# The last block's second layer as two column halves, each with its own finish and store

## The chip, the cores and the metric

The kernel runs on one core of a Trainium2 chip. The metric is the device time of one execution in microseconds (us), smaller is better. The core has a matrix engine (PE in the profile, with its weight loads listed apart as PEld), a vector engine (DVE), a scalar engine (ACT), a third elementwise engine that also issues loads (POOL), and a sync engine (SP) that here only issues DMA transfers. Each engine works through its own list of instructions in order; the lists meet at semaphores.

## The reference

Inputs are q, k and v of shape 4 x 8 x 768 x 64 (batch, heads, positions, head width) and the weights of one feed-forward layer. What is computed, cut to its core:

```python
scores = q @ k.T / sqrt(64)                       # per batch and head
keep   = (key < 4) | (0 <= query - key < 128)     # 4 sink keys, and a window of 128
a      = softmax(where(keep, scores, -1e9))
x      = (a @ v), heads side by side              # [4, 768, 512]
xn     = (x - mean(x)) / sqrt(var(x) + 1e-6) * g_ln
out    = x + relu(xn @ w_ch1) @ w_ch2             # 512 -> 2048 -> 512, float32
```

## The kernel before

The 4 x 768 positions are cut into 24 blocks of 128 rows, numbered t = 0 to 23. Each block goes through attention, and its normalized rows are laid out transposed in `xnt`. Four blocks make a group, so there are six groups, g = 0 to 5. For a group the feed-forward part has two layers:

- `m1` (the first layer): 16 tiles of 128 hidden units. Each takes four matmuls of 512 columns (the 512 rows of the group; group 0 does it in two parts of 256) into a PSUM bank `ph`, and one relu by ACT or DVE into a bf16 tile `h`.
- `m2` (the second layer): for each of the four blocks of the group, 16 matmuls that add up in one PSUM bank `pc` of 128 x 512 float32. A matmul takes a 128 x 128 piece of `h` as its weights and streams 512 columns of `w2s`. The 16 are added to the plan in four quanta of four. After them comes `fin`, one DVE instruction (scalar_tensor_tensor: `pc` times the row's factor `rsg`, plus the attention output `xt`) into the float32 tile `ot`, and `store`, one DMA of 256 KB that SP issues to the output.

The order of work is not written by hand. Every step is added to a `Planner` with a cost for each engine that could take it, its dependences, the buffers it takes and drops, and a priority; `plan.run` simulates this and picks the engine, the order on it and the buffer slots. Only the resulting order is issued; the costs are not times of the chip. PSUM banks come from a ring `pa` of four, output tiles from a ring `ot` of four.

At the end of the program nothing but group 5's second layer is left: blocks 20, 21, 22 and 23, one after the other on PE. After the last store SP waits, one instruction after the other, for each semaphore that its DMAs and the other engines have used; then the engines meet at a barrier and the program ends. Stores take eight DMA semaphores in rotation, and block 23's store is on the one that SP waits for second.

Lines of the profile that the text below uses: L603 the first layer's matmuls, L617 and L619 its relu on DVE and ACT, L634 the second layer's matmuls, L646 `fin`, L653 `store`, L517 the attention output's scaling (another scalar_tensor_tensor from PSUM, of 256 columns), L729 the program's end.

Of the kernel before, what the change touches and what calls it, by code (L numbers as in the profile page):

```python
# [7 lines left out]
FP32 = mybir.dt.float32  # L8
# [3 lines left out]
ALU = mybir.AluOpType  # L12
# [117 lines left out]
def kernel(  # L130
# [12 lines left out]
    nc = tc.nc  # L143
# [5 lines left out]
    DM = moe_w_ch1.shape[0]  # L149
    DH = moe_w_ch1.shape[1]  # L150
    NH1 = DH // 128
    NDM = DM // 128
    NT = B * RB
# [13 lines left out]
    plan = Planner(RINGS)  # L167
# [7 lines left out]
    def buf(ring, slot, shape, dtype, name):  # L175
        return pools[ring].tile(shape, dtype, name=name, tag=f"{ring}{slot}")

    def bank(slot, name):
        return buf("pa", slot, [128, 512], FP32, name)
# [14 lines left out]
    w2s = consts.tile([128, NH1, DM], BF16, name="w2s")  # L194
# [12 lines left out]
    xt = [consts.tile([128, DM], BF16, name=f"xt_{t}") for t in range(NT)]  # L207
# [50 lines left out]
    def rows_of(t):  # L258
        b, r = divmod(t, RB)
        return b, slice(128 * r, 128 * (r + 1))  # L260
# [23 lines left out]
    d_w1, d_w2 = {}, {}  # L284
# [28 lines left out]
    P = {}  # L313
# [13 lines left out]
    qkT, vs_t, E, ES, xc, xnt, mvg, rsg = {}, {}, {}, {}, {}, {}, {}, {}  # L327
    d_c, d_xn, d_rs, d_ks, d_vs = {}, {}, {}, {}, {}
# [253 lines left out]
    quanta = []  # L582
# [3 lines left out]
    h1 = {}  # L586
    d_h1 = {}
# [38 lines left out]
    def m2(g, base):  # L626
        m = None
        for ti, t in enumerate(GROUPS[g]):
            for qt in range(4):
                def f(e, *s, qt=qt, ti=ti, t=t):  # L630
                    if s:
                        P["pc", t] = bank(s[0], "pc")
                    for ht in range(4 * qt, 4 * qt + 4):
                        nc.tensor.matmul(P["pc", t], lhsT=h1[g, ht][:, 128 * ti:128 * (ti + 1)], rhs=w2s[:, ht, :],  # L634
                                         start=(ht == 0), stop=(ht == NH1 - 1))

                m = plan.add({"PE": .865}, [m, d_w2[qt]] + [d_h1[g, ht, t] for ht in range(4 * qt, 4 * qt + 4)], f,
                             (1, base, 4 * ti + qt), take=[("pa", ("pc", t), 1)] if qt == 0 else [],
                             drop=[("h1", g, ht) for ht in range(4 * qt, 4 * qt + 4)])

                quanta.append(m)

            def fin(e, s, ti=ti, t=t):
                ot = buf("ot", s, [128, DM], FP32, "ot")
                P["ot", t] = ot
                nc.vector.scalar_tensor_tensor(ot, in0=P["pc", t], scalar=rsg[g][:, ti:ti + 1], in1=xt[t],  # L646
                                               op0=ALU.mult, op1=ALU.add)

            o = plan.add({"DVE": .75}, [m, d_rs[g]], fin, (0, t, 9), take=[("ot", ("ot", t), 1)], drop=[("pc", t)])

            def store(e, t=t):
                bb, rows = rows_of(t)
                nc.sync.dma_start(out[bb, rows, :], P["ot", t])  # L653

            plan.add({"SP": .35}, [o], store, (0, t, 9), drop=[("ot", t)], land=.66)

    SPLIT = set(range(8))
    SPLIT_S = set(range(4))
# [26 lines left out]
    for i, (layer, g) in enumerate(SEQ):  # L685
        mark[layer, g] = len(quanta)
        (m1(g, i, SUBS.get(g)) if layer == 1 else m2(g, i))
# [46 lines left out]
```

## Time and profile before

| | us |
|---|---|
| median of 5 runs | 227.85 (227.63 to 227.87) |
| the profiled execution, its time | 227.87 |
| its span in the trace | 225.83 |
| PE busy | 219.0 (97% of the span) |
| DVE busy | 135.4 (60%) |
| ACT busy | 104.0 (46%) |
| POOL busy | 76.0 (34%) |

The profiled execution took 2.04 us more than the span that its instructions cover. The granted clock of PE is full (0.999) over the span. In the profile's views a group of instructions is shown with its count, its busy time and the mean duration of one; a matmul's duration runs from its start to the end of its result, so consecutive matmuls overlap, and the distance from start to start is the smaller number.

### The profile page before, as it was taken

How to read it: one execution, taken by the hardware profiler on the slowest of the kernel's cores; microseconds unless marked ns; L12 is line 12 of the kernel's file. 1: busy time of each engine (PE TensorE's matmuls, PEld its weight loads, DVE VectorE, ACT ScalarE, POOL GpSimd, SP SyncE). 2: the span in 40 equal slices, each digit the busy share in tenths (PEclk: the TensorE clock that was granted, in tenths of full speed). 3: DMA queues.
4: the chain of work that ended last, by engine and by line, in shares of the span. 5: the costliest groups of instructions: out<-in, count | busy, mean ns of one | idle time of the engine just before them, and what ended most of it. 6: DMA issues, size and time to landing. Idle time of an engine off the chain costs nothing.

```text
span 225.8 us, 4810 instructions
## 1 busy us (share of the span) xinstructions
PE 219.0 (97%) x1948; PEld 121.2 (54%) x1948; DVE 135.4 (60%) x398; ACT 104.0 (46%) x166; POOL 76.0 (34%) x92
## 2 busy tenths in 40 slices
PE   8999999999999999999999999999999999999992
PEld 7765887655455554454555544454554544444440
DVE  5787998789577988864756773744854712100121
ACT  2377788344368641166651247632077600376000
POOL 7994275691595241933089000100000010000000
PEclk9999999999999999999999999999999999999999
DMA  7999999999999999999979996203221021200111
GB/s 44 134 158 205 183 183 206 169 180 188 195 159 140 141 139 199 169 192 183 92 96 157 177 168 120 56 8 111 69 50 23 3 70 46 93 0 3 46 67 72
DMA packets 108709, 26.52 MB, mean 117 GB/s; under 512 B 101520, under 2 KB 105616, under 8 KB 108688
## 3 DMA queue, kind: packets, MB, share of 16 engines
q0 software_dynamic: 79104, 13.64, 81.0%
q1 hardware_dynamic: 29584, 12.59, 30.0%
q8 instruction: 15, 0.25, 0.4%
q14 instruction: 6, 0.05, 0.1%
HBM read 27.27 MB, written 6.29 MB: 149 GB/s over the span
## 4 chain that ended last, share of the span: by engine, by line
PE 82%; DMA 7%; POOL 5%; DVE 4%; issue 1%; ACT 0%; POOLq 0%; ACTq 0%
PE ph L603 35%; PE pc L634 34%; PE ps L406 5%; DMA w1s<-in_moe_w_ch_dram 4%; DMA qkT<-qkn 3%; PE po L501 2%; PE po L504 2%; POOL qkn L267 2%; PE po L496 2%; POOL qkn L272 2%; POOL vn L275 2%; PE pk L413 1%; DVE w1s L299 1%; PE pt L347 1%; DVE xt L517 1%
## 5 line engine op out<-in xcount | busy, mean ns | idle before, releaser
L603 PE MATMUL ph<-xnt,w1s 128*128 128x512 bf16 (+1 forms) x448 | 90.1, 349 | 0.4 <-DVE h L617 0.2
L634 PE MATMUL pc<-w2s,h 128*128 128x512 bf16 x384 | 88.6, 379 | 0.0
L619 ACT ACTIVATE h<-ph 128x512 bf16<-128x512 f32 (+1 forms) x84 | 45.9, 546 | 53.6 <-PE ph L603 53.2
L603 PEld LDWEIGHTS <-w1s 128*128 128x128 bf16 x448 | 41.5, 98 | 35.5 <-DVE w1s L299 0.6
L634 PEld LDWEIGHTS <-h 128*128 128x128 bf16 x384 | 35.8, 98 | 39.1
L435 ACT ACTIVATE e<-ps 128x1024 bf16<-128x1024 f32 (+1 forms) x48 | 43.7, 951 | 12.5 <-PE ps L406 12.5
L646 DVE SCALAR_TENSOR_TENSOR ot<-pc,rsg,xt 128x512 f32<-128x512 f32 x24 | 17.9, 747 | 38.9 <-PE pc L634 38.9
L548 POOL TENSOR_TENSOR rsg<-ve,eps_half 128x4 f32<-128x4 f32 x6 | 6.2, 1028 | 82.2 <-DVE ve L546 82.2
L267 POOL DMA_DIRECT2D qkn<-in_q_dram x24 | 22.1, 921 | 14.8 <-DMA qkT<-qkn 12.9
L444 DVE TENSOR_TENSOR e<-e,mask_std 128x1024 bf16<-128x1024 bf16 x28 | 18.9, 683 | 10.9 <-ACT e L435 10.9
L617 DVE TENSOR_SCALAR h<-ph 128x512 bf16<-128x512 f32 (+1 forms) x28 | 15.8, 569 | 13.7 <-PE ph L603 13.7
L272 POOL DMA_DIRECT2D qkn<-in_k_dram x24 | 21.8, 910 | 3.3 <-DMA w1s<-in_moe_w_ch_dram 1.8
L275 POOL DMA_DIRECT2D vn<-in_v_dram x24 | 22.0, 920 | 1.7 <-DMA w1s<-in_moe_w_ch_dram 1.7
L517 DVE SCALAR_TENSOR_TENSOR xt<-po,rc 128x256 bf16<-128x256 f32 x48 | 20.4, 424 | 1.7
L501 PE MATMUL po<-vn,e 128*128 128x65 bf16 x192 | 17.1, 193 | 0.0
L537 DVE BATCH_NORM_STATS2 st<-xt 128x6 f32<-128x512 bf16 x24 | 16.4, 683 | 0.0
L406 PEld LDWEIGHTS <-qkT 64*128 64x128 bf16 x352 | 9.9, 94 | 10.5 <-issue 7.8
L482 ACT ACTIVATE es<-pk 128x256 bf16<-128x256 f32 x16 | 6.1, 383 | 19.9 <-PE pk L413 19.8
L514 DVE RECIPROCAL rc<-po 128x4 f32<-128x4 f32 x48 | 8.5, 177 | 11.2 <-PE po L504 10.4
L406 PE MATMUL ps<-qkT 64*128 64x128 bf16 x352 | 14.7, 218 | 0.5 <-DMA qkT<-qkn 0.5
L501 PEld LDWEIGHTS <-e 128*128 128x128 bf16 x192 | 14.0, 97 | 2.1 <-DVE e L444 0.4
L504 PE MATMUL po<-vn,e 128*128 128x65 bf16 x160 | 14.9, 193 | 0.0
(66 smaller groups left out, 146.8 us busy)
## 6 DMA issues: line engine op xcount, KB each, us to landing
out_dram<-ot SPq DMA_DIRECT2D x24, 256.0 KB, 2.4
qkn<-in_q_dram POOLq DMA_DIRECT2D x24, 128.0 KB, 7.0
qkn<-in_k_dram POOLq DMA_DIRECT2D x24, 128.0 KB, 6.8
vn<-in_v_dram POOLq DMA_DIRECT2D x24, 128.0 KB, 7.4
w1s<-in_moe_w_ch_dram POOLq DMA_DIRECT2D x4, 512.0 KB, 10.8
w2s<-in_moe_w_ch_dram POOLq DMA_DIRECT2D x4, 512.0 KB, 10.7
qkT<-qkn SPq DMA_TRANSPOSE x16, 7.2
xnt<-xc SPq DMA_TRANSPOSE x16, 5.4
```

What stands on the lines that cost most here:

```text
L267: nc.gpsimd.dma_start(qn[t][:, 0], q[b, :, rows, :].rearrange("h p d -> p h d"))
L272: nc.gpsimd.dma_start(qn[t][:, 1], k[b, :, rows, :].rearrange("h p d -> p h d"))
L275: nc.gpsimd.dma_start(vn[:, t, :, 0:64], v[b, :, rows, :].rearrange("h p d -> p h d"))
L406: nc.tensor.matmul(ps[:, h2, hh, kb, :], lhsT=qkT[t - kb][rows, 1, hp, :], rhs=qkT[t][rows, 0, hp, :], start=(hh == 0 and kb == 0 and t no ...
L435: nc.scalar.activation(E[t, half][:, :, :, 0:nkb, :], P["ps", t, half][:, :, :, 0:nkb, :], AF.Exp, scale=scale)
L444: nc.vector.tensor_mul(ee[:, :, 0:w], ee[:, :, 0:w], m[:, 0:w].unsqueeze(1).to_broadcast([128, 4, w]))
L501: nc.tensor.matmul(po[:, hh, :], lhsT=ee[:, h % 2, hh // 2, 0, :], rhs=vn[:, t, h, :], start=(r < 2 and hh == 0), stop=(r == 0), skip_grou ...
L504: nc.tensor.matmul(po[:, hh, :], lhsT=ee[:, h % 2, hh // 2, 1, :], rhs=vn[:, t - 1, h, :], start=False, stop=True, skip_group_check=True)
L517: nc.vector.scalar_tensor_tensor(xt[t][:, 256 * half:256 * half + 256].rearrange("p (h d) -> p h d", h=4), in0=po[:, :, 0:64], scalar=1.0, ...
L603: nc.tensor.matmul(ph, lhsT=w1s[:, j, 128 * ht:128 * (ht + 1)], rhs=xnt[g][:, j, cols], start=(j == 0), stop=(j == NDM - 1))
L619: nc.scalar.activation(o, i, AF.Relu)
L634: nc.tensor.matmul(P["pc", t], lhsT=h1[g, ht][:, 128 * ti:128 * (ti + 1)], rhs=w2s[:, ht, :], start=(ht == 0), stop=(ht == NH1 - 1))
```

## The change

Only block 23, the last of all, is treated differently. Its 512 output columns are computed as columns 0 to 255 and then columns 256 to 511. Each half has its own PSUM bank, its own 16 matmuls of 256 columns (the same 16 weight tiles are loaded a second time), its own `fin` of 128 x 256 and its own store of 128 KB (128 rows of 1 KB each). Both halves write into the same `ot` tile, side by side. For all other blocks `halves` has one entry and the instructions are the same.

```diff
     def m2(g, base):
         m = None
         for ti, t in enumerate(GROUPS[g]):
-            for qt in range(4):
-                def f(e, *s, qt=qt, ti=ti, t=t):
+
+            halves = [(0, DM)] if t < NT - 1 else [(0, DM // 2), (DM // 2, DM)]
+            for c0, c1 in halves:
+                cols = slice(c0, c1)
+                for qt in range(4):
+                    def f(e, *s, qt=qt, ti=ti, t=t, cols=cols):
+                        if s:
+                            P["pc", t, cols.start] = bank(s[0], "pc")
+                        for ht in range(4 * qt, 4 * qt + 4):
+                            nc.tensor.matmul(P["pc", t, cols.start][:, cols], lhsT=h1[g, ht][:, 128 * ti:128 * (ti + 1)],
+                                             rhs=w2s[:, ht, cols], start=(ht == 0), stop=(ht == NH1 - 1))
+
+                    m = plan.add({"PE": .865 / len(halves)}, [m, d_w2[qt]] + [d_h1[g, ht, t] for ht in range(4 * qt, 4 * qt + 4)], f,
+                                 (1, base, 4 * ti + qt), take=[("pa", ("pc", t, c0), 1)] if qt == 0 else [],
+                                 drop=[("h1", g, ht) for ht in range(4 * qt, 4 * qt + 4)] if c1 == DM else [])
+
+                    quanta.append(m)
+
+                def fin(e, *s, ti=ti, t=t, cols=cols):
                     if s:
-                        P["pc", t] = bank(s[0], "pc")
...
+                        P["ot", t] = buf("ot", s[0], [128, DM], FP32, "ot")
+                    nc.vector.scalar_tensor_tensor(P["ot", t][:, cols], in0=P["pc", t, cols.start][:, cols],
+                                                   scalar=rsg[g][:, ti:ti + 1], in1=xt[t][:, cols],
+                                                   op0=ALU.mult, op1=ALU.add)
+
+                o = plan.add({"DVE": .75 / len(halves)}, [m, d_rs[g]], fin, (0, t, 9),
+                             take=[("ot", ("ot", t), len(halves))] if c0 == 0 else [], drop=[("pc", t, c0)])
+
+                def store(e, t=t, cols=cols):
+                    bb, rows = rows_of(t)
+                    nc.sync.dma_start(out[bb, rows, cols], P["ot", t][:, cols])
+
+                plan.add({"SP": .35}, [o], store, (0, t, 9), drop=[("ot", t)], land=.66 / len(halves))
```

In the instruction lists of the two kernels nothing else differs: ACT and POOL have the same instructions in the same order, PE has 16 more weight loads and matmuls at its end, DVE one more instruction, SP one more store. The first matmul of the second half carries a wait for a DVE semaphore, as its bank was block 20's `pc`. The second half's store is on the DMA semaphore that SP waits for third at the program's end, the first half's on the one that it waits for second.

More of the change, by code (lines that the diff above doesn't have):

```diff
@@ L628, in m2 @@
         for ti, t in enumerate(GROUPS[g]):
-            for qt in range(4):
-                def f(e, *s, qt=qt, ti=ti, t=t):
-                    if s:
-                        P["pc", t] = bank(s[0], "pc")
[L633 to L653, printed above, removed]
@@ L655, in m2 @@
-            plan.add({"SP": .35}, [o], store, (0, t, 9), drop=[("ot", t)], land=.66)
+            halves = [(0, DM)] if t < NT - 1 else [(0, DM // 2), (DM // 2, DM)]
[13 more added lines that the diff above has]
+                def fin(e, *s, ti=ti, t=t, cols=cols):
+                    if s:
+                        P["ot", t] = buf("ot", s[0], [128, DM], FP32, "ot")
[8 more added lines that the diff above has]
+                plan.add({"SP": .35}, [o], store, (0, t, 9), drop=[("ot", t)], land=.66 / len(halves))
```

## The prediction

> **What bounds the kernel now.** I began with the chain of waits that ended last, cut to the program's end, since the change touches nothing before block 23. Its columns are start, length and what ran (us).
>
> ```profile
> 199.86 7.99 PE ph L603 x37
> 207.85 13.83 PE pc L634 x64
> 221.67 0.02 issue
> 221.70 0.75 DVE ot L646
> ```
>
> PE is the bound up to 221.70. It streams all 64 matmuls of group 5's second layer without a gap: 13.83 us / 64 = 216 ns from start to start. After 221.70 PE has nothing left, and everything is one chain: `fin` (0.75), the store, SP's last waits, the barrier. The next view is the store's line in the last 4 us, with the time from issue to landing, and SP's instructions of the program's end right after that landing.
>
> ```profile
> L653 SPq DMA_DIRECT2D out_dram<-ot x1: 332/332/332, 222.5 to 222.5; - x1
> DMA to landing us min/median/max: 2.0/2.0/2.0
> ```
>
> ```profile
> L729 SPq EVENT_SEMAPHORE  x8: 27/28/28, 224.5 to 224.9; - x8
> L729 SPq DRAIN  x2: 7/7/7, 225.0 to 225.1; - x2
> ```
>
> So the tail is: `fin` 221.70 to 222.45, issue at 222.48, landing at 224.48, eight waits of SP from 224.50 to 224.93 (0.43 us / 7 = 61 ns apart), then the barrier until 225.83. From the last matmul's end to the program's end are 4.13 us in which PE does nothing. Inside the store's 2.0 us the DMA view of 222.4 to 226 us (40 slices of 0.09 us; busy share of the DMA engines in tenths, then GB/s) shows when data moves:
>
> ```profile
> DMA  0000000000899999951000000000000000000000
> GB/s 0 0 0 0 0 0 0 0 0 0 296 410 432 364 364 387 410 205 46 0 0 0 0 0 0 0 0 0 0 0 0 0 0 0 0 0 0 0 0 0
> DMA packets 144, 0.26 MB, mean 73 GB/s; under 512 B 16, under 2 KB 16, under 8 KB 144
> ```
>
> Data moves in slices 10 to 18, 223.30 to 224.11. Before it 0.82 us pass with nothing moving, after it 0.37 us. Only the middle part depends on the size. Last, the groups kept apart by shape, for the prices (busy us, mean ns of one):
>
> ```profile
> L634 PE MATMUL pc<-w2s,h 128*128 128x512 bf16 x384 | 88.6, 379 | 0.0
> L603 PE MATMUL ph<-xnt,w1s 128*128 128x256 bf16 x128 | 16.5, 273 | 0.4 <-DVE h L617 0.2
> L634 PEld LDWEIGHTS <-h 128*128 128x128 bf16 x384 | 35.8, 98 | 39.1
> L646 DVE SCALAR_TENSOR_TENSOR ot<-pc,rsg,xt 128x512 f32<-128x512 f32 x24 | 17.9, 747 | 38.9 <-PE pc L634 38.9
> L517 DVE SCALAR_TENSOR_TENSOR xt<-po,rc 128x256 bf16<-128x256 f32 x48 | 20.4, 424 | 1.7
> L617 DVE TENSOR_SCALAR h<-ph 128x512 bf16<-128x512 f32 x16 | 10.9, 685 | 13.5 <-PE ph L603 13.5
> L617 DVE TENSOR_SCALAR h<-ph 128x256 bf16<-128x256 f32 x12 | 5.0, 415 | 0.2 <-PE ph L603 0.2
> ```
>
> **The change, part by part.**
>
> *Matmuls (path).* 16 matmuls of 512 columns become 32 of 256. The trace has 256-column matmuls with a new weight tile each, in group 0's first layer. In the timeline (start, length):
>
> ```profile
> 26.88 2.78 PE L603 MATMUL ph<-xnt,w1s 128*128 128x256 bf16 x24 [0.20 <-DVE h L617]
> ...
> 29.49 0.39 PE L347 MATMUL pt<-ident,qkn 128*128 128x128 bf16 x4
> ```
>
> 24 of them fill 26.88 to 29.49: 109 ns from start to start, although each has its own weight load of 98 ns. The loads just fit under the streaming. So 32 x 109 = 3.49 us replace 16 x 216 = 3.46 us: +0.03. The last matmul starts later than its predecessor of before by about the 0.107 us that it is shorter in duration (379 against 273 ns), so PE's end moves only by that 0.03, to 221.73. From below I allow 0; from above see the third rival.
>
> *The first half (hidden).* Its `fin` can start 1.74 us (16 x 109) after block 22's result, at about 219.99, and takes under 0.5 us. DVE is free then: block 22's `fin` runs 218.24 to 218.99. Its store is issued at about 220.5, by an SP with nothing else to do, moves data at about 221.3 to 221.7 and lands by about 222.5 even at the full store's 2.0 us. The cover is the second half's matmuls (1.74 us) and its `fin`. The second half's store would issue at about 222.2 and move its first byte 0.82 us later, at 223.0, so the two transfers do not meet. Without this cover the halves' tails would be paid one after the other.
>
> *The wait at the second half's first matmul.* It waits for DVE to have emptied its bank. This is block 20's bank, emptied at 212.1 (its `fin` starts at 211.39), some 7.5 us earlier: 0. Queued behind it on PE are the last 15 matmuls, and for these the final `fin` and store wait, so a wait that really held would be paid in full (second rival).
>
> *The last `fin` (path).* 747 ns for 512 columns; for 256 no row has this form. The other scalar_tensor_tensor that reads PSUM, L517, takes 424 at 256 columns. L617 loses 270 ns from 512 to 256 columns; off 747 that leaves 477. I take the middle, 450: -0.30, with -0.27 and -0.33 as ends.
>
> [...] In the trace the fixed part shows, since L617 at half the columns still costs 61%. [...]
>
> *The last store (path).* 128 packets of 2 KB become 128 of 1 KB on the same 16 engines, eight each. Before, eight took about 0.70 us (the stage of 0.81 less its ragged ends), 88 ns each. If the rate of some 390 GB/s holds, 1 KB takes 44 ns and the saving is 8 x 44 = 0.35. If a packet has a fixed part it is less: the profile's queue table gives the hardware queue 29584 packets in 30.0% of 16 engines' span, 1084 us. The 24 stores' 3072 packets at 88 ns take 270 of these, so that the other 26,100, of 241 bytes on average, took 31 ns each. Between 31 ns at 241 bytes and 88 at 2048, 1 KB comes to 56 ns: a saving of 8 x 32 = 0.26. I take -0.30. As no row has 1 KB packets on this queue, the far end is 0.
>
> [...]
>
> *SP's last waits (path).* The final landing now releases the third of SP's waits instead of the second; the second, for the first half's store, is over by then. One step of 61 ns fewer stands after the landing: -0.06 (0 if the order does not matter).
>
> *The sum.* +0.03 - 0.30 - 0.30 - 0.06 = -0.63 us. Against the profiled execution's own time, 225.83 span + 2.04 around it = 227.87, this gives 227.24; that execution lay 0.02 above the median of the runs, so 227.22. The ends: 0 - 0.33 - 0.35 - 0.06 = -0.74 (227.11), and 0.03 - 0.27 - 0 - 0 = -0.24 (227.61).
>
> **The rivals.** *The store's half saves nothing*: if 1 KB packets take as long as 2 KB ones, or if landing goes from these 2.0 us to the 2.4 that is the median of all 24 stores, the tail keeps its transfer, and the sum is -0.33 to 0, 227.5 to 227.85. For it: no such packet in the trace. Against: small packets on this queue are plainly shorter, and the slower landings are in stages where loads and transposes run, while the tail has none.
>
> *The second half waits for the first's `fin`*: if the bank were not free, PE would stand for that `fin` plus the drain of the last matmul, 0.45 + (0.273 - 0.109) = 0.61, and the sum is -0.02: no change, 227.83. Against: the bank is block 20's.
>
> *Slower*: the weight loads come out from under the matmuls. With 256 columns PE has 109 ns to hide 98; if load and stream alternated, each matmul would cost 98 + 109 = 207 and the 32 would take 6.62 us, +3.17 against now, net +2.5: 230.4. It decides from 109 + 0.66/32 = 130 ns per matmul on, where the gain is gone. For it: L603's 256-column group has a mean busy time of 16.5/128 = 129 ns. Against: that mean includes the drains of short bursts, and the burst of 24 above holds 109.
>
> **How the numbers follow.** About 0.2% (0.46 us) is what a measurement of this kernel can tell from no change. My forecast lies 0.17 us beyond it, with chance 0.77. The first rival has 0.14 and the second 0.04, both within 0.2%; slower has 0.05. The range runs from a little under the best sum, 227.05, to the worst one, 227.6, which takes in part of the first rival.
>
> **What would show it.** In the changed profile: 32 second-layer matmuls 109 ns apart, ending at about 221.73; a last `fin` of 128x256 at 0.42 to 0.48 us; two stores of 128 KB, the second issued at about 222.2 and landing about 1.7 us later; seven waits of SP after it; a span of about 225.2. I am wrong if PE stands between the halves, if matmuls lie over 130 ns apart, or if the second store still takes 2.0 us.

## The result, and the profile after

The changed kernel takes 227.22 us (median of 47 runs, 226.55 to 228.37) against 227.87 (85 runs, 226.71 to 229.19). The ratio is 0.9975, with a 95% interval of 0.9966 to 0.9984: about 0.57 us faster, between 0.36 and 0.77 (the medians themselves lie 0.65 apart). The forecast was 0.63 us.

The profiled execution took 226.80 us, with a span of 224.69. That is 1.14 under the span of before, and only half of it belongs to the change: the first matmul of group 5's second layer starts at 207.12 instead of 207.68, and up to there both kernels issue the same instructions. Single executions differ by as much. From here on a stage is therefore compared that begins at the same event, the start of block 22's `fin`, and ends with the span: 225.83 - 218.24 = 7.59 us before, 224.69 - 217.68 = 7.01 after, a gain of 0.57. One profiled execution of each kernel is compared, but such a stage repeats well: from block 21's `fin` to block 22's, where all kernels here but one (E5) do the same, it takes 3.453 or 3.454 us in each of nine traces. Least steady is the time from the last data to the landing, 0.34 to 0.38 us in all of them but E7.

The chain that ended last, at its end (start, length, what ran):

```profile
199.95 7.34 PE ph L603 x34
207.28 13.87 PE pc L638 x80
221.15 0.03 issue
221.18 0.48 DVE ot L650
```

PE is still gapless: 80 matmuls now. The timeline from block 22's result on shows the two `fin`s, the second half's 1.75 us after the first's, with the waits for PE in brackets:

```profile
217.68 0.75 DVE L650 SCALAR_TENSOR_TENSOR ot<-pc,rsg,xt 128x512 f32<-128x512 f32 x1 [2.70 <-PE pc L638]
...
219.43 0.48 DVE L650 SCALAR_TENSOR_TENSOR ot<-pc,rsg,xt 128x256 f32<-128x256 f32 x1 [0.99 <-PE pc L638]
221.18 0.48 DVE L650 SCALAR_TENSOR_TENSOR ot<-pc,rsg,xt 128x256 f32<-128x256 f32 x1 [1.26 <-PE pc L638]
```

The DMA view of the second half's store, over a stretch of the same length and with the same slices of 0.09 us as before, beginning 0.09 before its issue at 221.69:

```profile
DMA  0000000000599961000000000000000000000000
GB/s 0 0 0 0 0 0 0 0 0 0 182 353 353 330 205 34 0 0 0 0 0 0 0 0 0 0 0 0 0 0 0 0 0 0 0 0 0 0 0 0
out_dram<-ot SPq DMA_DIRECT2D x1, 128.0 KB, 1.7
```

Data moves in 6 slices where it took 9, after the same pause of 0.83 us. The rate is somewhat lower (353 at most, against 364 to 432 GB/s in the full slices). Over a longer stretch, 219 to 225 us in slices of 0.15, the transfers of block 22 and of the two halves are three separate ones:

```profile
DMA  0189995000018950000000039920000000000000
```

And SP's instructions at the program's end, from the last landing on:

```profile
L735 SPq EVENT_SEMAPHORE  x7: 27/28/28, 223.4 to 223.8; - x7
L735 SPq DRAIN  x2: 7/7/7, 223.9 to 223.9; - x2
```

Seven waits follow the landing, where it was eight before; the first of them is the one that the landing releases. Step by step, in us:

| step | before | after | difference | forecast |
|---|---|---|---|---|
| block 22's `fin` starts to block 23's last `fin` starts | 3.453 | 3.494 | +0.041 | +0.03 |
| last `fin` | 0.750 | 0.484 | -0.266 | -0.30 |
| its end to the issue | 0.028 | 0.028 | 0 | 0 |
| issue to first data | 0.831 | 0.828 | -0.003 | 0 |
| data moves | 0.830 | 0.518 | -0.312 | -0.30 |
| last data to landing | 0.347 | 0.384 | +0.037 | 0 |
| landing to the end | 1.346 | 1.275 | -0.071 | -0.06 |
| sum | 7.585 | 7.011 | -0.574 | -0.63 |

### The profile page after: what moved, and what is told of

Its sections match the earlier page's. It is cut to its first block, busy times and chain, and to the rows that moved or that the text cites. A ratio compares the mean times of both kernels' runs of the same rounds, so it can differ in the third digit from the quotient of the medians.

```text
span 224.7 us, 4845 instructions
## 1 busy us (share of the span) xinstructions
PE 218.7 (97%) x1964; PEld 122.6 (55%) x1964; DVE 135.5 (60%) x399; ACT 103.9 (46%) x166; POOL 75.9 (34%) x92
## 4 chain that ended last, share of the span: by engine, by line
PE 88%; DVE 4%; POOL 3%; DMA 3%; issue 1%; POOLq 0%
PE pc L638 37%; PE ph L603 35%; PE ps L406 5%; DMA vn<-in_v_dram 3%; PE po L501 2%; PE po L504 2%; PE po L496 2%; PE pk L413 1%; POOL qkn L267 1%; DVE w1s L299 1%; POOL qkn L272 1%; PE pt L347 1%; DVE xt L517 1%; PE px L559 1%; DVE xc L529 1%
## 5 line engine op out<-in xcount | busy, mean ns | idle before, releaser
L638 PE MATMUL pc<-w2s,h 128*128 128x512 bf16 (+1 forms) x400 | 88.6, 371 | 0.0
L638 PEld LDWEIGHTS <-h 128*128 128x128 bf16 x400 | 37.4, 98 | 37.8
L650 DVE SCALAR_TENSOR_TENSOR ot<-pc,rsg,xt 128x512 f32<-128x512 f32 (+1 forms) x25 | 18.2, 726 | 38.4 <-PE pc L638 38.4
L617 DVE TENSOR_SCALAR h<-ph 128x512 bf16<-128x512 f32 (+1 forms) x28 | 15.8, 569 | 13.5 <-PE ph L603 13.5
L517 DVE SCALAR_TENSOR_TENSOR xt<-po,rc 128x256 bf16<-128x256 f32 x48 | 20.4, 424 | 1.7
L501 PE MATMUL po<-vn,e 128*128 128x65 bf16 x192 | 17.1, 193 | 0.4 <-DMA vn<-in_v_dram 0.4
L501 PEld LDWEIGHTS <-e 128*128 128x128 bf16 x192 | 14.1, 97 | 2.1 <-DVE e L444 0.4
L504 PE MATMUL po<-vn,e 128*128 128x65 bf16 x160 | 14.9, 193 | 0.0
```

Of the source, the lines that this page charges most:

```text
L501: nc.tensor.matmul(po[:, hh, :], lhsT=ee[:, h % 2, hh // 2, 0, :], rhs=vn[:, t, h, :], start=(r < 2 and hh == 0), stop=(r == 0), skip_grou ...
L504: nc.tensor.matmul(po[:, hh, :], lhsT=ee[:, h % 2, hh // 2, 1, :], rhs=vn[:, t - 1, h, :], start=False, stop=True, skip_group_check=True)
L517: nc.vector.scalar_tensor_tensor(xt[t][:, 256 * half:256 * half + 256].rearrange("p (h d) -> p h d", h=4), in0=po[:, :, 0:64], scalar=1.0, ...
L638: nc.tensor.matmul(P["pc", t, cols.start][:, cols], lhsT=h1[g, ht][:, 128 * ti:128 * (ti + 1)], rhs=w2s[:, ht, cols], start=(ht == 0), sto ...
```

## The experiments

The diffs below are against the changed kernel and cut to the lines that matter; the comments in them are not in the kernels. All stages are of one profiled execution, from block 22's `fin` to the end of the span unless said otherwise: 7.59 before, 7.01 with the change. Medians of E1 to E4 stand beside 227.59 for the kernel before on the same chip (35 runs), those of E5 to E8 beside 227.54 (29 runs).

| run | median us | ratio (95%) | stage us |
|---|---|---|---|
| E1 one store | 227.74 | 1.0005 (0.9985 to 1.0026) | 7.35 |
| E2 `fin` and store alone | 227.62 | 1.0006 (0.9990 to 1.0022) | 7.45 |
| E3 same bank | 227.90 | 1.0013 (0.9996 to 1.0031) | 7.75 |
| E4 quarters | 226.56 | 0.9964 (0.9946 to 0.9982) | 6.68 |
| E5 last group | 226.93 | 0.9970 (0.9951 to 0.9988) | see below |
| E6 semaphore order | 226.89 | 0.9971 (0.9950 to 0.9992) | 6.62 |
| E7 384 and 128 | 226.95 | 0.9962 (0.9946 to 0.9977) | 6.81 |
| E8 three parts, order | 226.27 | 0.9938 (0.9917 to 0.9959) | 6.37 |

My theory was that three separate terms behind the last matmul shrink, and that this is free only because the first half lies under the second half's matmuls. The rivals were that one term alone carries the gain, that smaller pieces are enough without a cover, and, from the prediction, the wait for a bank and the weight loads.

**E1: two `fin`s, one store.**

```diff
-                plan.add({"SP": .35}, [o], store, (0, t, 9), drop=[("ot", t)], land=.66 / len(halves))
+                if c1 == DM:     # and store() writes all 512 columns of ot
+                    plan.add({"SP": .35}, [o], store, (0, t, 9), drop=[("ot", t)], land=.66)
```

> Two halves of matmuls and two fins for block 23, but one store of 256 KB after the second fin, as before. The stage measured is from the start of block 22's fin to the end of the span: 7.59 us before, 7.01 with the change. My theory (three separate path terms: last fin 0.27, last transfer 0.31, one step of SP's last waits 0.07, less 0.04 of matmuls) expects the fin's and the matmuls' terms alone: a stage of 7.36, some 0.23 below before. The rival that the gain is the transfer's alone (the second store half as long) expects 7.6, no gain. The rival that the smaller last fin brings all of it expects 7.0.

The stage is 225.85 - 218.50 = 7.35. In the timeline, block 22's `fin` and the last one:

```profile
218.50 0.75 DVE L650 SCALAR_TENSOR_TENSOR ot<-pc,rsg,xt 128x512 f32<-128x512 f32 x1 [2.70 <-PE pc L638]
...
221.99 0.48 DVE L650 SCALAR_TENSOR_TENSOR ot<-pc,rsg,xt 128x256 f32<-128x256 f32 x1 [1.26 <-PE pc L638]
```

The last `fin` takes 0.484, the store 2.01 from issue to landing as before, and eight waits follow. So `fin` and matmuls give 0.23 and the store with its semaphore 0.34; neither carries the gain alone. In the medians the 0.23 does not show: a difference under about 0.2%, 0.46 us, is lost in their noise, and the interval of E1 takes in both 0 and the 0.23. The same holds for the small differences of E2 and E3.

**E2: whole matmuls, `fin` and store in halves.**

```diff
-                for qt in range(4):
+                for qt in range(4) if c0 == 0 else ():   # 16 matmuls of 512 columns, one bank
```

> The matmuls of block 23 stay whole (16 of 512 columns, one bank), but its fin and its store are cut into two column halves. My theory (the halves pay only because the first half's fin and store lie under the second half's matmuls) expects both fins after the last matmul, 0.97 us instead of 0.75, a second store 1.0 us after the result that lands 1.73 later, and one step of waits less: a stage of 7.4 to 7.5, most of the gain gone. The rival that smaller last pieces are enough by themselves expects the same stage as the change, 7.0, or 0.04 less as no matmuls are added.

The stage is 7.45, as my theory had it. In the timeline both `fin`s run together after PE's end:

```profile
222.20 0.88 DVE L650 SCALAR_TENSOR_TENSOR ot<-pc,rsg,xt 128x256 f32<-128x256 f32 x2 [2.70 <-PE pc L638]
```

They take 0.88 instead of 0.75, so the second store is issued later than the single one of before would be, and of the gain 0.13 is left. Of the 0.44 lost against the change, most is this: from the start of the `fin` that follows PE's end to the issue of the last store it takes 0.94, not 0.51. What is lost is the time of a second `fin`, hardly that of a second store: the two stores are in flight together and land 0.47 apart, though each takes over 1.7 from issue to landing. The cover makes the difference, not the smaller piece.

**E3: the second half in the first half's bank.**

```diff
                         if s:
-                            P["pc", t, cols.start] = bank(s[0], "pc")
+                            if cols.start:
+                                s = (P["slot", t],)          # the first half's slot
+                            P["slot", t] = s[0]
+                            P["pc", t, cols.start] = bank(s[0], "pc")
...
-                    m = plan.add({"PE": .865 / len(halves)}, [m, d_w2[qt]] + [d_h1 ...
+                    m = plan.add({"PE": .865 / len(halves)}, [m, d_w2[qt]] + ([o] if c0 and qt == 0 else []) + [d_h1 ...
```

> As the change, but the second half uses the bank of the first half, so its first matmul waits until the first half's fin has read it. My theory and the second rival's price agree on what such a wait costs: drain of the first half's last matmul 0.16, its fin 0.48 and a semaphore's way, 0.65 to 0.75 in all: a stage of 7.65 to 7.75, no better than the 7.59 of before. If instead the wait costs little (the matrix engine works ahead), the stage stays near 7.0.

The stage is 7.75. In the timeline PE stands between the halves, and DVE's read of the bank is what ends it:

```profile
219.87 0.48 DVE L653 SCALAR_TENSOR_TENSOR ot<-pc,rsg,xt 128x256 f32<-128x256 f32 x1 [1.00 <-PE pc L641]
220.41 1.91 PE L641 MATMUL pc<-w2s,h 128*128 128x256 bf16 x16 [0.58 <-DVE ot L653]
```

From the last start of the first half to the first start of the second are 849 ns instead of 109: the wait costs 0.74 us, more than the whole gain. The change avoids it only because the second half has a bank that was empty.

**E4: four quarters.**

```diff
-            halves = [(0, DM)] if t < NT - 1 else [(0, DM // 2), (DM // 2, DM)]
+            halves = [(0, DM)] if t < NT - 1 else [(c, c + 128) for c in range(0, DM, 128)]
```

> Block 23 in four quarters of 128 columns instead of two halves: 64 matmuls of 128 columns, four fins, four stores of 64 KB. If a weight load of 98 ns must be hidden under one matmul, as the prediction's third rival has it, 64 matmuls cannot go faster than 98 ns each: 6.27 us in place of 3.49, and with 0.13 less for the last fin, 0.15 for the transfer and 0.12 for the waits the stage becomes 9.4. If weight loads overlap with each other (the trace of before has bursts of short matmuls, each with its own weights, only 30 to 57 ns apart), they go 56 ns apart, 3.58 us in all, and the stage becomes 6.7, better than the change.

The stage is 6.68, the second alternative. The groups by shape, from 217 us on:

```profile
L638 PE MATMUL pc<-w2s,h 128*128 128x128 bf16 x64 | 3.7, 219 | 0.0
L638 PEld LDWEIGHTS <-h 128*128 128x128 bf16 x64 | 3.7, 98 | 0.2
L650 DVE SCALAR_TENSOR_TENSOR ot<-pc,rsg,xt 128x128 f32<-128x128 f32 x4 | 1.4, 352 | 1.8 <-PE pc L638 1.6
```

64 matmuls of 128 columns lie 56 ns apart although each has its own weight load of 98 ns: 64 x 98 would be 6.3 us, and the loads' busy time is 3.7, so they overlap each other. The mean duration of a load was no bound on the rate here (98 ns against 56). The trace of before had this already: at 22.45 to 22.66 us the attention's matmuls (L501 and L504) start some 30 ns apart, each with a weight load of 96 to 100 ns. Cutting the last block finer gains a further 0.33.

**E5: all four blocks of the last group in halves.**

```diff
-            halves = [(0, DM)] if t < NT - 1 else [(0, DM // 2), (DM // 2, DM)]
+            halves = [(0, DM)] if t < 20 else [(0, DM // 2), (DM // 2, DM)]
```

> All four blocks of the last group in halves, not block 23 alone. Stage measured: from the first second-layer matmul of group 5 to the end of the span, 18.15 us before, 17.57 with the change. My theory (a split costs 0.035 us of matmuls wherever it stands, and pays only at the end, where nothing follows) expects 3 x 0.035 more, and 3 x 0.06 less because three more stores move the last one to a DMA semaphore that SP waits for later: 17.5, as good as the change. A rival that each split saves of itself, as each block's result leaves sooner, expects another 0.57 per block, or at least a visible part of it: below 17.0.

The stage from the first second-layer matmul is 225.347 - 207.864 = 17.48, as expected from the two prices (17.5); blocks 20, 21 and 22 gain nothing by their own split. The chain has 128 matmuls in 13.99 us, where the change had 80 in 13.87:

```profile
208.03 13.99 PE pc L638 x128
222.01 0.02 issue
222.04 0.48 DVE ot L650
```

**E6: the last store on the last semaphore.**

```diff
+                for sc_ in [slice(c, c + 128) for c in range(0, DM, 128)] if t in (20, 21) else [cols]:
                     ...                                       # store(), for the columns sc_
```

> As the change, but blocks 20 and 21 store their 512 columns in four pieces each. Their data is the same, and the six stores more only move block 23's last store to the DMA semaphore that SP waits for last of the eight. Stage from block 22's fin to the end of the span: 7.01 with the change. My theory (each wait of SP behind the last landing costs 61 ns) expects 6 x 61 = 0.37 less: 6.64. The rival that these waits are hidden, because the barrier waits for something else, expects 7.0; a rival that more stores in flight delay the last one expects over 7.0.

The stage is 6.62. The waits of SP at its queue's end (who waited for whom, us, times, longest), first of the change, then of E6:

```profile
SPq L735 <- DMA out_dram<-ot: 1.3, 1, 1.3
```

```profile
SPq L736 <- DMA out_dram<-ot: 0.9, 1, 0.9
```

SP spends the time on its other waits first and reaches the one that counts 0.4 us later, so that after the landing only one wait is left. Of the 0.39 gained, 0.36 lies between landing and end, 60 ns for each of the six steps; the other 0.03 lies between issue and landing. This also confirms the term of the semaphore's place in the sum, at one step.

**E7: 384 and 128 columns.**

```diff
-            halves = [(0, DM)] if t < NT - 1 else [(0, DM // 2), (DM // 2, DM)]
+            halves = [(0, DM)] if t < NT - 1 else [(0, 384), (384, DM)]
```

> Block 23 in two unequal parts, 384 and 128 columns. By the runs so far: matmuls 16 x 163 + 16 x 56 = 3.50 us (3.49 with halves), last fin 0.35 (0.48), last transfer of 64 KB some 0.15 shorter, waits as with the change: a stage of 7.01 - 0.13 - 0.15 = 6.73. What could spoil it: the first part's fin (about 0.6) and its 192 KB must go under only 0.9 us of matmuls; if the two transfers meet, the last one is late by up to 0.3 and the stage stays near 7.0.

The stage is 6.81, 0.08 over my number. The DMA view from 221.9 us on shows why: the two stores' transfers touch.

```profile
DMA  0000000000889999449830000000000000000000
GB/s 0 0 0 0 0 0 0 0 0 0 290 324 393 393 307 324 137 137 284 239 86 0 0 0 0 0 0 0 0 0 0 0 0 0 0 0 0 0 0 0
```

The first store's data ends where the second's begins, and the second lands 1.64 us after its issue, against 1.56 for the store of the same size in E4, whose predecessor was long done; most of the difference, 0.06, lies between the last data and the landing. That the contact is the cause is inferred from this pair, not isolated.

**E8: the fastest version.** Parts of 256, 192 and 64 columns, and five more stores earlier, so that the last one is on the semaphore that SP waits for last.

```diff
-            halves = [(0, DM)] if t < NT - 1 else [(0, DM // 2), (DM // 2, DM)]
+            halves = [(0, DM)] if t < NT - 1 else [(0, 256), (256, 448), (448, DM)]
...
+                cuts = {20: [0, 128, 256, 384, 512], 21: [0, 128, 256, 512]}.get(t, [c0, c1])
```

> A version meant to be fastest: block 23 in parts of 256, 192 and 64 columns, and blocks 20 and 21 stored in four and three pieces, so that the last store is on the DMA semaphore that SP waits for last of the eight. By the runs so far: matmuls 16 x (109 + 82 + 30) = 3.54 us, last fin about 0.28, last transfer of 32 KB about 0.2 us, six steps of waits less than the change: a stage of 6.2 to 6.3, about 1.3 under before. If matmuls of 64 columns are bound by their weight loads (98 ns in place of 30) it is 1.1 us more; if packets of 256 bytes move no faster than those of 512, 0.1 more.

The stage is 6.37, 1.22 under before, and the median 226.27 is the lowest of all, 0.62% under before by the ratio. The intervals of E4, E7 and E8 overlap, so that E8 is the fastest is read from the stages. The weight loads do not bind even at 64 columns (29 ns from start to start), and packets of 256 bytes are faster than those of 512 (18 against 27 ns). What stands between 6.37 and my number is SP:

```profile
220.61 0.71 PE L638 MATMUL pc<-w2s,h 128*128 128x192 bf16 x17
...
220.90 0.75 DVE L650 SCALAR_TENSOR_TENSOR ot<-pc,rsg,xt 128x192 f32<-128x192 f32 x2 [0.83 <-PE pc L638]
221.34 0.33 SPq L661 DMA_DIRECT2D out_dram<-ot  x1
```

SP is still issuing the second part's store (221.34 for 0.33 us) when the last `fin` ends at 221.65, and the last store leaves at 221.77, 0.09 later than right after its `fin`. Issued right behind another, it also takes 0.39 to issue, not 0.33, and its first data moves 0.90 after its start, not 0.83. DVE does not hold it up: the two last `fin`s (0.417 and 0.283) stand in one row of the timeline, but the last one begins at 221.36, 0.04 after the last matmul's end as with the change, and the one before it is over at 221.31.

## Why the prediction was right

The mechanism is the one named: PE does not stop, and what follows it is shorter. That the median meets the forecast to the hundredth (227.22) is luck: the gain is known to 0.2 us only, and the stages put it at 0.57 where 0.63 was forecast.

- *Matmuls.* +0.03 foreseen, +0.041 measured; 109 ns apart as in group 0. The reason given for it was wrong in part: the loads do not "just fit under the streaming". E4 and E8 show them overlapping each other at 56 and 29 ns. The third rival's threshold of 130 ns and its 0.207 us per matmul were therefore no real danger, and the 30 ns of L501 and L504 in the trace of before could have told so.
- *The first half.* Hidden as forecast: its store lands at 221.64, before the second is issued at 221.69. E2 shows the price without this cover: 0.44 of the 0.57 is lost. But the halves' tails are then not "paid one after the other": only the two `fin`s are, while the two stores overlap.
- *The wait at the second half's first matmul.* 0, as it held nothing. The second rival's price was too low, 0.61 against 0.74 in E3: it had the `fin` 0.03 too short and left out the way of the semaphores between PE and DVE, 0.09 in all.
- *The last `fin`.* The middle of the two rows (450) was too low; 484 is close to the 477 that came from L617's slope, and L517's 424 was the wrong neighbour. The runs give `fin` 283, 352, 417, 484, 617 and 750 ns at 64, 128, 192, 256, 384 and 512 columns: 1.04 ns per column on a fixed 217. L617's two rows (685 and 415 ns) had pointed to such a fixed part. With it both halves' durations add up to 0.97 us instead of 0.75, and E2, where nothing hides them, has 0.88 from the start of the first to the end of the second.
- *The last store.* -0.30 foreseen, -0.312 measured in the data and +0.037 in the landing, -0.275 together. The +0.037 does not come with the size: E5 and E6 have 0.35 and 0.34 there with the same 128 KB; its cause is open. A packet of 1 KB takes 47 to 48 ns in the trace where one of 2 KB takes 86, between the two values of 44 and 56. The 56 was too high because it rests on a mean: the 256-byte packets of before take 30 ns on average but 18 in the median, and in E8's last store 18 as well; from 18 the same working gives 48. The first rival, that half a store saves nothing, falls with this. The fixed time of one more transfer cost nothing here: the first half's store runs from 219.94 to 221.64, under the second half's matmuls and its `fin` (to 221.66); in E2 the two transfers' fixed times lie under each other (landings 0.47 us apart, with over 1.7 from issue to landing for each).
- *SP's last waits.* -0.06 foreseen, -0.071 measured, and E6 shows 0.06 for each of six steps.

The terms add to -0.574 in the profile against the -0.63 forecast. The `fin` (0.034) and the landing (0.037) fell short, and the other terms give 0.015 back. Two small slips changed nothing: the 4.13 us without PE run from the last `fin`'s start (from the last matmul's end it is 4.17), and the queue's other packets are 26,512, not 26,100.

## What to carry to other kernels

Where the last thing in a program is one result's evacuation and store, cut that result so that all but a small last piece is evacuated and stored while the matrix engine still works; cut elsewhere it only costs matmul overhead (0.12 us for three blocks in E5). Give each piece its own free PSUM bank (waiting for one cost 0.74 us in E3), and see that the issuing queue (0.09 us in E8) and, as far as one pair of runs tells, the transfers (0.08 us in E7) of two pieces do not meet. Then look at the instructions after the last landing: waits that are satisfied anyway should stand before the one that counts, not after it (0.36 us in E6).

## What the runs showed of the hardware

- Weight loads of 98 ns each do not keep matmuls 98 ns apart: with new weights for each, 128 columns ran at 56 ns (E4) and 64 columns at 29 ns (E8) from start to start.
- A store's packet on this queue took 86, 67, 47, 36, 27 and 18 ns (medians) at 2048, 1536, 1024, 768, 512 and 256 bytes, which is close to 8 ns and 0.038 ns per byte; a row of 1 KB costs about a tenth more per byte than one of 2 KB.
- A wait of SP on a semaphore that has already arrived still costs 61 ns, and before the change seven of them stood behind the one for the last landing.
- A store that SP issued right behind another took 0.38 to 0.43 us to issue (E2, E6, E8); with a pause before it, a store in this last stretch took 0.33 in all runs but one (0.51, once in E5).
